# Splitting the second product's result straight from PSUM, with a scale bounded ahead of time

## The chip, the core and the metric

The kernel runs on one core of a Trainium2 chip. The metric is the device time of one execution in microseconds (us); the kernel before took 1235.76 us, the median of three timed runs (1233.34 to 1237.47).

The engines of the core are TensorE (PE in the profile; its weight loads are PEld), VectorE (DVE), ScalarE (ACT), GpSimd (POOL) and SyncE (SP, which issues nearly all DMAs here). Each has a queue of its own that it works through in order.

## The reference: what is computed

Attention over 4 batches of 448 tokens with 12 heads of 64, and on its output two gated products one after the other, 1792 tokens in all. The inputs are float64 for the weights and fp32 accuracy is wanted of the result.

```
q_n, k_n = rmsnorm(q, g_q), rmsnorm(k, g_k)
attn = softmax(q_n @ k_n^T / 8)
x = (attn @ v), heads side by side           # [1792, 768]

a = x @ w_a                                  # [1792, 1536]
b = x @ w_b
y = (a * b) @ w_out                          # [1792, 768]      <- the second product

h = y @ w2_in                                # [1792, 2048]
g = max(h, 0) + alpha * min(h, 0)
out = g @ w2_out                             # [1792, 768]
```

## The kernel before

**Split products.** PE multiplies in fp16. To keep fp32's accuracy, every operand is stored as two fp16 halves, hi and lo, after scaling by a power of two; a product is three matmuls (`prod`, L746): hi by hi, hi by lo, lo by hi. Each matmul here is 128x128 by 128x448. Weights are split the same way once (`w_load`, `w_convert`, `w_scale`, `w_split`, L618 to L710) as they are first used, their halves stored to a scratch tensor in HBM, and loaded from there in later batches. `w_scale` takes a weight chain's sum of squares and derives from it a power-of-two scale and its inverse; the inverses of all six chains of `w_out` stand in `inv["y"]`, a [128, 6] tile.

**Stages.** Work goes in stages, one letter for the product and one digit for the batch: `a` (x by w_a and w_b, 24 chains), `y` (a*b by w_out, 6 chains of 36 matmuls in two halves), `h` (y by w2_in, 16 chains of 18 matmuls) and `o` (g by w2_out, 6 chains). The order is a0 y0 h0 o0 a1 y1 a2 h1 o1 y2 a3 h2 y3 o2 h3 o3. So only y0 is followed directly by the stage that needs its result; after y1, y2 and y3 another stage comes in between. Attention of the next batch is woven into these stages at fixed rates (`RATE`); its score matmuls write tile `s`, its output matmuls tile `x`. The first batch's stages also convert and split the weights. A tile framework's scheduler arranges the instructions on each engine.

**The second product, `stage_y` (L809 to L835).** A chain's sum is in a PSUM tile `ps` from `new_ps()` (three buffers in turn). After the chain's second half ACT copies it to an fp32 tile in SBUF, scaled by the weight's inverse scale (L820), and squares that into a bf16 tile `sq` (L821). When all six chains are done, PE multiplies a matrix of ones by the six squares (L827), which adds the squares over all rows, into a PSUM tile `norm`. DVE takes the maximum over the tokens (L829) and derives the batch's scale `sy` and its inverse `iy` with three small integer operations (`power`, L109 to L120). Only then `split` (L758) makes the halves of each chain m: ACT the hi half, `Copy` with scale `sy` (L760), and DVE the lo half, `t * sy - hi` (L761). Before h0 the six splits follow at once; in the other batches they are put on the list `tasks` and taken one by one in the next stage (`next_w`).

**What uses it.** `stage_h` reads `Y[b, kk]`; its first chain needs all six. In `stage_o` GpSimd multiplies the inverse scales together into `cum` (L892 to L895), among them `iy` of the batch.

**A similar scale.** `h_scales` (L682) already does for w2_in's chains what the change now does for w_out's too: it takes the largest of the inverse scales as one common scale, so that the halves of `g` can be made as soon as a chain is done (flag `state["cgf"]`).

Of the kernel before, what the change touches and what calls it, by code (L numbers as in the profile page):

```python
# [19 lines left out]
def attention_gated_mlps_kernel(  # L20
# [15 lines left out]
    nc = tc.nc  # L36
# [32 lines left out]
    def slot32(name):  # L69
        return slot_p.tile([128, S], F32, tag="slot", name=name)  # L70
# [10 lines left out]
    gT = const.tile([128, 1], F32, name="gT")  # L81
    gkT = const.tile([128, 1], F32, name="gkT")
    ones = const.tile([128, 128], F32, name="ones")
    onesb = const.tile([128, 128], BF16, name="onesb")
    gbc = const.tile([128, D], F32, name="gbc")
    gkb = const.tile([128, D], F32, name="gkb")
    gm = const.tile([128, 1], F32, name="gm")
# [3 lines left out]
    cg = const.tile([128, 1], F32, name="cg")  # L91
    icg = const.tile([128, 1], F32, name="icg")
    cgf = const.tile([128, KF2], F32, name="cgf")
    ssv = const.tile([KP, B, NP], F32, name="ssv")
    ssab = const.tile([128, 2, KF], F32, name="ssab")
    sx, ix, sab, iab, sy, iy, cum = [
        const.tile([128, B], F32, name=n) for n in ("sx", "ix", "sab", "iab", "sy", "iy", "cum")
    ]
    inv = {
        "a": const.tile([128, 2 * KF], F32, name="inv_a"),  # L100
# [5 lines left out]
    def mm(o, a, b, first, last):  # L106
        nc.tensor.matmul(out=o, lhsT=a, rhs=b, start=first, stop=last)  # L107
# [42 lines left out]

    def setup0():
        nc.vector.memset(ones, 1.0)
        nc.vector.memset(onesb, 1.0)
        for t in p16:
            nc.vector.memset(t, 0.0)

# [376 lines left out]
        )  # L533
        P[g] = None

    state = dict(pin=True, cgf=False)
    preps = (prep2, prep3, prep4)
    preps_f = (prep2f, prep3f, prep4f)

# [126 lines left out]
    def w_scale(u):  # L666

        if u not in squares:
            return
        kind, n, part = stream[u]  # L670
        _, parts, _ = CHAINS[kind]
        chains = GROUP[kind]
        us = range(u - parts * chains + 1, u + 1)
        sc = sm_p.tile([128, 2], F32, tag="sc", name="sc")[:, 0:chains]
        iv = inv[kind][:, n - chains + 1:n + 1]
        power(total(squares.pop(u), len(us), chains), sc, iv)
        for x in us:
            scales[x] = sc[:, (x - us[0]) // parts:(x - us[0]) // parts + 1]
        if (kind, n) == ("h", KF2 - 1):
            h_scales()  # L680

    def h_scales():  # L682

        mx = sm_p.tile([128, 1], F32, tag="mh", name="mh")
        ci = sm_p.tile([128, 1], F32, tag="mh", name="ci")
        nc.vector.tensor_reduce(out=mx, in_=inv["h"], axis=AX.X, op=ALU.max)
        nc.vector.tensor_scalar(
            ci.bitcast(I32), mx.bitcast(I32), -1.0, float(254 << 23), op0=ALU.mult, op1=ALU.add
        )
# [68 lines left out]
    def split(t, s, name):  # L758
        x = slot(name)
        nc.scalar.activation(out=x[:, 0], in_=t, func=AF.Copy, scale=s)  # L760
        nc.vector.scalar_tensor_tensor(  # L761
            out=x[:, 1], in0=t, scalar=s, in1=x[:, 0], op0=ALU.mult, op1=ALU.subtract
        )
        return x
# [42 lines left out]
            tasks.extend((lambda i=i: one(i)) for i in range(n))  # L807

    def stage_y(b):  # L809
        raw, sq = {}, [slot_p.tile([128, 2, S], BF16, tag="slot", name=f"sq{b}_{i}") for i in range(KD // 2)]  # L810
        for m in range(KD):
            ps = new_ps()[:, 0:S]
            for kh in range(2):
                yield
                hw = unit()
                for kk in range(KD):
                    prod(ps, hw, kk, AB[b, kh * KD + kk], kh + kk == 0, kh == 1 and kk == KD - 1)
                if kh == 1:
                    raw[m] = t = slot32(f"y32_{b}_{m}")
                    nc.scalar.activation(out=t, in_=ps, func=AF.Copy, scale=inv["y"][:, m:m + 1])  # L820
                    nc.scalar.activation(out=sq[m // 2][:, m % 2], in_=t, func=AF.Square)  # L821
                next_w()
        for f in range(KF):
            AB.pop((b, f))
        ps = ps_x.tile([128, 512], F32, tag="x", name="norm")[:, 0:S]
        for m in range(KD):
            mm(ps, onesb, sq[m // 2][:, m % 2], m == 0, m == KD - 1)  # L827
        t = sm_p.tile([128, 1], F32, tag="mx", name="mx")
        nc.vector.tensor_reduce(out=t, in_=ps, axis=AX.X, op=ALU.max)  # L829
        power(t, sy[:, b:b + 1], iy[:, b:b + 1])  # L830

        def one(m):
            Y[b, m] = split(raw.pop(m), sy[:, b:b + 1], f"y{b}_{m}")

        after(stages_after("y", b) == "h", one, KD)  # L835

    def stage_h(b):
        raw = {}
# [30 lines left out]
    def stage_o(b):  # L869
        NT, PT = 4, S // 4  # L870
        k = CHAINS["o"][2]

        def finish(m, ps):
            t = tmp()

            nc.scalar.activation(  # L876
                out=t.rearrange("q (p c) -> q c p", c=NI),
                in_=ps.rearrange("q (c p) -> q c p", c=NI),
                func=AF.Copy, scale=inv["o"][:, m:m + 1],
            )  # L880
            po = new_ps()[:PT].rearrange("p (t f) -> p t f", t=NT)
            for i in range(NT):
                nc.tensor.transpose(po[:, i, :], t[:, i * PT:(i + 1) * PT], ident)  # L883
            ob = ob_p.tile([PT, NT, 128], F32, tag="ob", name="ob")
            nc.scalar.activation(out=ob, in_=po, func=AF.Copy, scale=cum[:PT, b:b + 1])
            nc.sync.dma_start(
                out=out[b * S:(b + 1) * S, m * 128:(m + 1) * 128].rearrange("(t p) f -> p t f", t=NT),
                in_=ob,
            )

        c = cum[:, b:b + 1]
        nc.gpsimd.tensor_tensor(c, ix[:, b:b + 1], iab[:, b:b + 1], op=ALU.mult)  # L892
        nc.gpsimd.tensor_tensor(c, c, iy[:, b:b + 1], op=ALU.mult)
        nc.gpsimd.tensor_tensor(c, c, icg, op=ALU.mult)
        nc.gpsimd.tensor_tensor(c, c, ix[:, b:b + 1], op=ALU.mult)  # L895
        late = None
        for m in range(KD):
            ps = new_ps()[:, 0:S]
            for part in range(4):
                yield  # L900
                hw = unit()
                for kk in range(k):
                    prod(
                        ps, hw, kk, G[b, part * k + kk],
                        part + kk == 0, part == 3 and kk == k - 1,
                    )
# [93 lines left out]
```

## Time and profile before

| | |
|---|---|
| timed, median of 3 | 1235.76 us (1233.34 to 1237.47) |
| profiled execution: time | 1237.6 us |
| profiled execution: span from first to last instruction | 1235.8 us |
| mean granted TensorE clock | 0.981 |
| 24 squares, L821, ACT | 576 ns each (median) |
| 24 norm matmuls, L827 by way of L107, PE | 352 ns each as modelled; their starts are closer |
| 4 maxima, L829, DVE | 623 ns each (median) |

A matmul's row gives a duration from its start to its modelled end, while the next one starts well before that; what a matmul costs in a stream is the distance from start to start. "Idle before" in a timeline row is the time the engine stood still before it, with what released it. A stretch is given by its limits in us from the span's start.

### The profile page before, as it was taken

The page shows a single profiled execution, that of the slowest core. Times are in us where ns is not written, and L with a number is a line of the kernel's source. Part 1 is how long each engine was busy: PE and PEld are TensorE (multiplying, and loading weights), DVE is VectorE, ACT ScalarE, POOL GpSimd, SP SyncE. Part 2 cuts the span into 40 slices and gives each one's busy share as a digit, 9 for nine tenths or more (in the row PEclk, how much of TensorE's full clock was granted, in tenths as well). Part 3 has the DMA queues.
Part 4 walks back from the last instruction along what each step waited for, and adds up shares of the span by engine and source line. Part 5 has one row for each costly group of instructions (what it writes and reads, how often), then busy time and mean ns, then how long its engine had stood idle before and what let it go on. Part 6 is the DMA issues. An engine that isn't in the chain of part 4 may idle for free.

```text
span 1235.8 us, 18195 instructions
## 1 busy us (share of the span) xinstructions
PE 1169.1 (95%) x6574; PEld 599.5 (49%) x6574; DVE 677.4 (55%) x1455; ACT 738.8 (60%) x1504; POOL 10.4 (1%) x32
## 2 busy tenths in 40 slices
PE   6997998989988999979999999999999999999998
PEld 4553554444534444435455454545555555554554
DVE  7898999889899667666551465331111440102400
ACT  7998999999889767676643465553221441213311
POOL 1000000000000000000000000000000000000000
PEclk9997999999999999989999999999999999999999
DMA  7558999999999999897854737876333333344343
GB/s 196 162 169 214 306 338 323 298 299 304 287 262 287 238 253 240 190 225 166 219 145 125 167 104 170 191 189 158 102 116 116 115 117 107 110 144 129 98 128 89
DMA packets 311243, 234.68 MB, mean 190 GB/s; under 512 B 175440, under 2 KB 284496, under 8 KB 311152
## 3 DMA queue, kind: packets, MB, share of 16 engines
q1 hardware_dynamic: 311040, 233.43, 71.7%
q8 instruction: 52, 0.85, 0.3%
q0 software_dynamic: 112, 0.07, 0.2%
q14 instruction: 39, 0.32, 0.1%
HBM read 155.79 MB, written 32.24 MB: 152 GB/s over the span
## 4 chain that ended last, share of the span: by engine, by line
PE 54%; DMA 2%; ACT 1%; DVE 1%; issue 0%; SPq 0%; ACTq 0%; DVEq 0%
PE p L107 49%; PE s L107 2%; PE x L107 2%; DMA pT<-p 2%; PE p L883 1%; ACT t L876 0%; PE norm L107 0%; ACT p L479 0%; ACT pf L434 0%; DVE nm L417 0%; SPq L486 0%; DVE ab L782 0%; DVE p L480 0%; DVE kr L332 0%; DVE qr L326 0%
## 5 line engine op out<-in xcount | busy, mean ns | idle before, releaser
L107 PEld LDWEIGHTS <-w 128*128 128x128 f16 x4896 | 476.7, 99 | 477.0 <-issue 49.7
L107 PE MATMUL p<-x,w 128*128 128x448 f16 x1728 | 336.8, 354 | 2.1 <-ACT t L779 2.0
L107 PE MATMUL p<-g,w 128*128 128x448 f16 x1152 | 229.5, 356 | 5.5 <-DVE g L844 2.1
L107 PE MATMUL p<-y,w 128*128 128x448 f16 x1152 | 224.7, 356 | 3.5 <-ACT y L760 3.2
L107 PE MATMUL p<-ab,w 128*128 128x448 f16 x864 | 170.8, 358 | 1.3 <-ACT ab L760 1.3
L417 DVE TENSOR_REDUCE nm<-s 128x2 f32<-128x896 f32 x84 | 91.1, 1085 | 41.7 <-PE s L107 41.3
L480 DVE SCALAR_TENSOR_TENSOR p<-pf,ri,p 128x448 f16<-128x448 f32 x126 | 84.4, 680 | 34.3 <-ACT p L479 34.0
L479 ACT ACTIVATE p<-pf,ri 128x448 f16<-128x448 f32 x126 | 81.4, 663 | 36.0 <-DMA pT<-p 28.1
L434 ACT ACTIVATE pf<-s,nm,esc 128x448 f32<-128x448 f32 x126 | 90.1, 719 | 1.3
L858 DVE SCALAR_TENSOR_TENSOR t<-t,al,p 128x448 f32<-128x448 f32 x55 | 37.3, 678 | 96.5 <-ACT t L857 96.5
L782 DVE SCALAR_TENSOR_TENSOR ab<-p,inv_a,t 128x448 f32<-128x448 f32 x48 | 32.5, 677 | 96.0 <-PE p L107 95.9
L706 DVE SCALAR_TENSOR_TENSOR w<-wf,sc,w 128x768 f16<-128x768 f32 (+1 forms) x76 | 70.2, 926 | 4.5 <-ACT w L705 4.1
L876 ACT ACTIVATE t<-p,inv_o 128x448 f32<-128x448 f32 x24 | 25.6, 1067 | 76.4 <-PE p L107 76.4
L785 ACT ACTIVATE junk<-ab 128x448 bf16<-128x448 f32 x48 | 27.4, 572 | 68.0 <-DVE ab L782 68.0
L650 DVE SCALAR_TENSOR_TENSOR wf<-raw,wf 128x768 int32<-128x768 int32 (+1 forms) x76 | 65.8, 867 | 0.5
L705 ACT ACTIVATE w<-wf,sc 128x768 f16<-128x768 f32 (+1 forms) x76 | 65.5, 866 | 0.0
L644 ACT ACTIVATE wf<-raw 128x768 f32<-128x768 f32 (+1 forms) x76 | 63.3, 838 | 1.6 <-DVE w L706 1.2
L658 ACT ACTIVATE junk<-wf 128x768 bf16<-128x768 f32 (+1 forms) x76 | 58.9, 775 | 2.9 <-DVE wf L650 2.5
L857 ACT ACTIVATE t<-p 128x448 f32<-128x448 f32 x55 | 29.7, 541 | 48.4 <-PE p L107 48.2
L843 ACT ACTIVATE g<-t,cgf 128x448 f16<-128x448 f32 x55 | 36.7, 668 | 34.6 <-DVE t L858 34.6
L107 PE MATMUL s<-kT,qT 128*64 128x448 f16 x252 | 50.2, 376 | 6.1 <-ACT pf L434 2.8
L844 DVE SCALAR_TENSOR_TENSOR g<-t,cgf,g 128x448 f16<-128x448 f32 x55 | 37.5, 682 | 29.6 <-ACT g L843 29.5
(140 smaller groups left out, 1065.1 us busy)
## 6 DMA issues: line engine op xcount, KB each, us to landing
w<-sc_a SPq DMA_DIRECT2D x72, 384.0 KB, 3.2
w<-sc_h SPq DMA_DIRECT2D x48, 384.0 KB, 3.0
w<-sc_o SPq DMA_DIRECT2D x72, 256.0 KB, 3.1
w<-sc_y SPq DMA_DIRECT2D x36, 384.0 KB, 3.2
raw<-in_moe_w_in_dram SPq DMA_DIRECT2D x16, 768.0 KB, 7.8
raw<-in_moe_w_out_dram SPq DMA_DIRECT2D x24, 512.0 KB, 5.9
raw<-in_moe_w_a_dram SPq DMA_DIRECT2D x12, 768.0 KB, 7.4
raw<-in_moe_w_b_dram SPq DMA_DIRECT2D x12, 768.0 KB, 7.5
```

The costliest lines, as they stand in the source:

```text
L107: nc.tensor.matmul(out=o, lhsT=a, rhs=b, start=first, stop=last)
L417: nc.vector.tensor_reduce(out=nm, in_=ps[:, :, 0:S], axis=AX.X, op=ALU.max, negate=True)
L434: nc.scalar.activation(out=pf, in_=ps[:, j, 0:S], func=AF.Exp, bias=nm[:, j:j + 1], scale=scale[j], accum_out=su[:, j:j + 1],)
L479: nc.scalar.activation(out=t[:, 0, :, 0:KP], in_=pf, func=AF.Copy, scale=r)
L480: nc.vector.scalar_tensor_tensor(out=t[:, 1, :, 0:KP], in0=pf, scalar=r, in1=t[:, 0, :, 0:KP], op0=ALU.mult, op1=ALU.subtract,)
L644: nc.scalar.activation(out=t, in_=hi.bitcast(F32), func=AF.Prelu, scale=2.0 ** -112, alpha=-(2.0 ** 32))
L650: nc.vector.scalar_tensor_tensor(out=ti, in0=lo, scalar=29, in1=ti, op0=ALU.logical_shift_right, op1=ALU.bitwise_or)
L658: nc.scalar.activation(out=junk(768, size(kind)), in_=t, func=AF.Square, accum_out=sums[0][:, j:j + 1])
L705: nc.scalar.activation(out=w[:, 0], in_=t, func=AF.Copy, scale=s)
L706: nc.vector.scalar_tensor_tensor(out=w[:, 1], in0=t, scalar=s, in1=w[:, 0], op0=ALU.mult, op1=ALU.subtract)
L844: nc.vector.scalar_tensor_tensor(out=x[:, 1], in0=t, scalar=cgf[:, f:f + 1], in1=x[:, 0], op0=ALU.mult, op1=ALU.subtract,)
L858: nc.vector.scalar_tensor_tensor(out=t, in0=t, scalar=al[:, f:f + 1], in1=ps, op0=ALU.mult, op1=ALU.add)
```

## The change

The batch's scale `sy` is no longer measured from y. `power` makes each scale from a norm, and the scales of a*b and of w_out's chains already bound the size of each sum in PSUM. So one constant factor 2^-17 and the ratio of each chain's inverse scale to the largest of them (`cyf`, [128, 6]) are enough to split, and `iy` is one [128, 1] value for all batches. `cyf` is made once, when the last of w_out's chains has its scale, which happens in the course of y0. From then on a chain's halves are taken from its PSUM tile as soon as the chain is done. The chains of y0 that end before that are copied to SBUF in fp32 (without scale) and split later, one beside each chain that follows. Squares, norm matmuls, their maximum, the tile `onesb` and the fp32 copies go.

```diff
@@ in w_scale
         if (kind, n) == ("h", KF2 - 1):
-            h_scales()
-
-    def h_scales():
+            ci, mx = common("h")
+            nc.vector.tensor_scalar(cgf, inv["h"], ci, cg, op0=ALU.mult, op1=ALU.mult)
+            nc.gpsimd.tensor_tensor(icg, icg, mx, op=ALU.mult)
+            state["cgf"] = True
+        if (kind, n) == ("y", KD - 1):
+            ci, mx = common("y")
+            nc.vector.tensor_scalar(cyf, inv["y"], ci, 2.0 ** -17, op0=ALU.mult, op1=ALU.mult)
+            nc.vector.tensor_scalar(iy, mx, 2.0 ** 17, None, op0=ALU.mult)
+            state["cyf"] = True
+
+    def common(kind):
 
         mx = sm_p.tile([128, 1], F32, tag="mh", name="mh")
         ci = sm_p.tile([128, 1], F32, tag="mh", name="ci")
-        nc.vector.tensor_reduce(out=mx, in_=inv["h"], axis=AX.X, op=ALU.max)
+        nc.vector.tensor_reduce(out=mx, in_=inv[kind], axis=AX.X, op=ALU.max)
         nc.vector.tensor_scalar(
             ci.bitcast(I32), mx.bitcast(I32), -1.0, float(254 << 23), op0=ALU.mult, op1=ALU.add
         )
-        nc.vector.tensor_scalar(cgf, inv["h"], ci, cg, op0=ALU.mult, op1=ALU.mult)
-        nc.gpsimd.tensor_tensor(icg, icg, mx, op=ALU.mult)
-        state["cgf"] = True
+        return ci, mx
@@ stage_y
-        raw, sq = {}, [slot_p.tile([128, 2, S], BF16, tag="slot", name=f"sq{b}_{i}") for i in range(KD // 2)]
+        raw = {}
+
+        def one(m):
+            Y[b, m] = split(raw.pop(m), cyf[:, m:m + 1], f"y{b}_{m}")
+
         for m in range(KD):
             ps = new_ps()[:, 0:S]
...
-                if kh == 1:
-                    raw[m] = t = slot32(f"y32_{b}_{m}")
-                    nc.scalar.activation(out=t, in_=ps, func=AF.Copy, scale=inv["y"][:, m:m + 1])
-                    nc.scalar.activation(out=sq[m // 2][:, m % 2], in_=t, func=AF.Square)
                 next_w()
+            if state["cyf"]:
+                raw[m] = ps
+                for x in sorted({m, min(raw)}):
+                    one(x)
+            else:
+                raw[m] = t = slot32(f"y32_{b}_{m}")
+                nc.scalar.copy(t, ps)
+        for x in sorted(raw):
+            one(x)
         for f in range(KF):
             AB.pop((b, f))
-        ps = ps_x.tile([128, 512], F32, tag="x", name="norm")[:, 0:S]
-        for m in range(KD):
-            mm(ps, onesb, sq[m // 2][:, m % 2], m == 0, m == KD - 1)
-        t = sm_p.tile([128, 1], F32, tag="mx", name="mx")
-        nc.vector.tensor_reduce(out=t, in_=ps, axis=AX.X, op=ALU.max)
-        power(t, sy[:, b:b + 1], iy[:, b:b + 1])
-
-        def one(m):
-            Y[b, m] = split(raw.pop(m), sy[:, b:b + 1], f"y{b}_{m}")
-
-        after(stages_after("y", b) == "h", one, KD)
@@ stage_o
-        nc.gpsimd.tensor_tensor(c, c, iy[:, b:b + 1], op=ALU.mult)
+        nc.gpsimd.tensor_tensor(c, c, iy, op=ALU.mult)
```

How the rows stand then, at two places. First DVE between y0 and h0. In the rows below `mx`, `pw`, `sy` and `iy` are the maximum of the norms and what `power` makes of it, `wf` is a weight being converted, `w` its halves, `qr` and `kr` are the attention's inputs of a later batch, `t`, `r` and `m` its row norms, `y_0` to `y_5` the halves of the six chains. Before:

```order
L829 TENSOR_REDUCE mx<-norm 128x1
L326 TENSOR_TENSOR qr<-qr,r 128x448
L332 SCALAR_TENSOR_TENSOR kr<-kr,r 112x512
L329 TENSOR_TENSOR qr<-qr,gbc 128x448
L114 TENSOR_SCALAR pw<-mx 128x1
L650 SCALAR_TENSOR_TENSOR wf<-raw,wf 128x768
L117 TENSOR_SCALAR sy<-pw 128x1
L120 TENSOR_SCALAR iy<-pw 128x1
L647 TENSOR_SCALAR wf<-wf 128x768
L114 TENSOR_SCALAR pw<-tot 128x2
L650 SCALAR_TENSOR_TENSOR wf<-raw,wf 128x768
L761 SCALAR_TENSOR_TENSOR y_0_3331<-y_0_0_2724,sy,y_0_3331 128x448
```

And after, up to the last of the six lo halves:

```order
L712 SCALAR_TENSOR_TENSOR w_3352<-wf,sc,w_3352 128x768
L259 TENSOR_TENSOR t<-r 128x30
L650 SCALAR_TENSOR_TENSOR wf<-raw,wf 128x768
L260 SCALAR_TENSOR_TENSOR t<-t,m 128x30
L115 TENSOR_SCALAR pw<-tot 128x2
L263 SCALAR_TENSOR_TENSOR r<-t,r 128x30
L647 TENSOR_SCALAR wf<-wf 128x768
L259 TENSOR_TENSOR t<-r 128x30
L118 TENSOR_SCALAR sc<-pw 128x2
L121 TENSOR_SCALAR inv_h<-pw 128x2
L260 SCALAR_TENSOR_TENSOR t<-t,m 128x30
L767 SCALAR_TENSOR_TENSOR y_5_3320<-p,cyf,y_5_3320 128x448
```

Before, all six lo halves stood behind the maximum and its scale, in a row of six of which the first is shown; after, `y_5` reads the PSUM tile `p`, the other five stand further ahead among y0's work, and the attention's `qr` and `kr` rows come behind it.

Second PE at the same hand-over. `ab` is a half of a*b, `w` a weight, `norm` and `onesb` the tiles of the norm, `s` the attention's scores, `tot` the sum of a weight's squares. Before, the end of the norm and the way to h0's first matmul, with most score rows in between left out by taking two pieces:

```order
L107 LDWEIGHTS onesb
L107 MATMUL norm<-sq_2_2649,onesb 128x448
L107 LDWEIGHTS qS
L107 MATMUL s<-kT,qS 64x448
L107 LDWEIGHTS onesb
L107 MATMUL norm<-sq_2_2649,onesb 128x448
L107 LDWEIGHTS qT
L107 MATMUL s<-kT,qT 64x448
```

```order
L107 LDWEIGHTS qS
L107 MATMUL s<-kT,qS 64x448
L107 MATMUL tot<-ss,ones 128x2
L107 LDWEIGHTS qS
L107 MATMUL s<-kT,qS 64x448
L107 LDWEIGHTS w_3196
L107 MATMUL p<-y_0_3331,w_3196 128x448
```

And after, y0's last matmul and h0's first:

```order
L108 LDWEIGHTS w_3143
L108 MATMUL p<-ab_11_2642,w_3143 128x448
L108 MATMUL tot<-ss,ones 128x2
L108 LDWEIGHTS w_3198
L108 MATMUL p<-y_0_2954,w_3198 128x448
```

The sixteen score matmuls (two steps of eight) that stood between y0 and h0 now stand behind h0's first chain and further on; h0's first chain of 18 follows y0 directly.

## Rows read from the trace of the kernel before

**Rows 1.** The page, part 1: busy us, share of the span, instructions.

```profile
PE 1169.1 (95%) x6574; PEld 599.5 (49%) x6574; DVE 677.4 (55%) x1455; ACT 738.8 (60%) x1504; POOL 10.4 (1%) x32
```

**Rows 2.** Busy time by stretch: length, then each engine's us (instructions), PEclk, DMA share, GB/s.

```profile
218.60:261.40 42.80, 39.99 (x221) 20.10 (x221) 35.59 (x67) 41.34 (x78) 0.24 (x1) 0.96 1.08 295
261.40:270.40 9.00, 9.00 (x54) 4.82 (x54) 8.72 (x22) 8.34 (x18) 0.00 (x0) 1.00 1.09 277
270.40:279.05 8.65, 4.37 (x27) 2.12 (x26) 8.63 (x24) 8.28 (x17) 0.37 (x1) 0.89 1.16 336
279.05:284.90 5.85, 5.81 (x18) 2.41 (x18) 5.83 (x11) 5.24 (x11) 0.00 (x0) 0.58 0.97 235
284.90:325.00 40.10, 40.10 (x232) 21.06 (x231) 34.58 (x65) 34.47 (x67) 0.00 (x0) 1.00 1.08 307
325.00:342.00 17.00, 16.78 (x95) 8.46 (x94) 17.00 (x40) 16.86 (x38) 1.61 (x3) 1.00 1.09 294
342.00:352.90 10.90, 6.55 (x35) 2.60 (x29) 10.76 (x19) 10.90 (x24) 0.00 (x0) 0.97 0.98 261
553.20:605.20 52.00, 52.00 (x300) 25.52 (x300) 34.62 (x75) 35.03 (x74) 0.00 (x0) 0.96 0.81 186
...
1017.70:1058.70 41.00, 41.00 (x218) 21.23 (x217) 1.36 (x2) 7.26 (x12) 0.00 (x0) 1.00 0.36 103
```

**Rows 3.** Timeline of PE, y0 to h0: start us, us, instruction, [idle before <-releaser].

```profile
270.58 0.38 PE L107 MATMUL s<-kT,qT 128*64 128x448 f16 x2
270.79 0.36 PE L107 MATMUL s<-kT,qS 128*64 128x448 f16 x2
...
271.45 1.12 PE L107 MATMUL norm<-sq,onesb 128*128 128x448 bf16 x5
...
279.09 6.16 PE L107 MATMUL p<-y,w 128*128 128x448 f16 x19 [3.23 <-ACT y L760]
```

**Rows 4.** Timeline of DVE at the same place.

```profile
261.42 1.09 DVE L417 TENSOR_REDUCE nm<-s 128x2 f32<-128x896 f32 x1 [0.60 <-PE s L107]
...
274.24 0.61 DVE L829 TENSOR_REDUCE mx<-norm 128x1 f32<-128x448 f32 x1
274.77 0.61 DVE L326 TENSOR_TENSOR qr<-qr,r 128x448 f32<-128x448 f32 x1
...
277.37 0.14 DVE L117 TENSOR_SCALAR sy<-pw 128x1 int32<-128x1 int32 x1
```

**Rows 5.** Tile y: count, duration ns min/median/max, first and last start, forms.

```profile
L820 ACT ACTIVATE y<-p,inv_y x24: 608/633/635, 227.8 to 1058.8; 128x448 f32<-128x448 f32 x24
L821 ACT ACTIVATE sq<-y x24: 559/576/578, 229.0 to 1059.4; 128x448 bf16<-128x448 f32 x24
L760 ACT ACTIVATE y<-y,sy x24: 652/654/668, 278.4 to 1064.3; 128x448 f16<-128x448 f32 x24
L761 DVE SCALAR_TENSOR_TENSOR y<-y,sy,y x24: 673/677/685, 279.1 to 1065.2; 128x448 f16<-128x448 f32 x24
```

**Rows 6.** The same view of tile x.

```profile
L530 ACT ACTIVATE x<-x,sx x6: 633/657/684, 38.0 to 122.1; 128x448 f16<-128x448 f32 x6
L531 DVE SCALAR_TENSOR_TENSOR x<-x,sx,x x6: 672/675/684, 38.9 to 123.1; 128x448 f16<-128x448 f32 x6
```

**Rows 7.** Timeline of PE after y1, at a2's start.

```profile
608.26 0.35 PE L107 MATMUL norm<-sq,onesb 128*128 128x448 bf16 x1 [1.38 <-ACT sq L821]
```

**Rows 8.** DVE's groups from 218 to 270: busy us, mean ns | idle before, releaser.

```profile
L706 DVE SCALAR_TENSOR_TENSOR w<-wf,sc,w 128x768 f16<-128x768 f32 x10 | 10.1, 1011 | 1.3 <-ACT w L705 1.0 <-DMA sc_y<-w 0.2
L650 DVE SCALAR_TENSOR_TENSOR wf<-raw,wf 128x768 int32<-128x768 int32 x10 | 9.6, 955 | 0.2
...
L647 DVE TENSOR_SCALAR wf<-wf 128x768 int32<-128x768 int32 x10 | 5.5, 553 | 1.2 <-ACT wf L644 1.2
```

**Rows 9.** SP's waits from 218 to 353: us in total, times, longest.

```profile
SPq L709 <- DVE w L706: 6.8, 3, 5.1
```

**Rows 10.** ACT's waits in y1, from 553 to 606.

```profile
ACT y L820 <- PE p L107: 2.4, 2, 1.9
```

More of the change, by code (lines that the diff above doesn't have):

```diff
@@ L83, in attention_gated_mlps_kernel @@
     ones = const.tile([128, 128], F32, name="ones")
-    onesb = const.tile([128, 128], BF16, name="onesb")
     gbc = const.tile([128, D], F32, name="gbc")
@@ L93, in attention_gated_mlps_kernel @@
     cgf = const.tile([128, KF2], F32, name="cgf")
+    cyf = const.tile([128, KD], F32, name="cyf")
+    iy = const.tile([128, 1], F32, name="iy")
     ssv = const.tile([KP, B, NP], F32, name="ssv")
     ssab = const.tile([128, 2, KF], F32, name="ssab")
-    sx, ix, sab, iab, sy, iy, cum = [
-        const.tile([128, B], F32, name=n) for n in ("sx", "ix", "sab", "iab", "sy", "iy", "cum")
+    sx, ix, sab, iab, cum = [
+        const.tile([128, B], F32, name=n) for n in ("sx", "ix", "sab", "iab", "cum")
     ]
@@ L152, in setup0 @@
         nc.vector.memset(ones, 1.0)
-        nc.vector.memset(onesb, 1.0)
         for t in p16:
@@ L534, in pv_out @@
         P[g] = None
-    state = dict(pin=True, cgf=False)
+    state = dict(pin=True, cgf=False, cyf=False)
     preps = (prep2, prep3, prep4)
```

## The prediction

> **What bounds the kernel now.** I read, in this order: the page's busy shares, the busy time by stretch, the idle places of TensorE (PE) in its timeline, and then the timelines of the two engines it waits for there. PE is busy 95% of the span, VectorE (DVE) 55%, ScalarE (ACT) 60% [rows 1]. So a matmul taken out of a stretch where PE never stops is worth its full time, and work taken off DVE or ACT is worth nothing unless PE waits for it there. The stretches differ, however [rows 2]. In stage y0 (218.6 to 270.4) ACT is busy 41.34 of 42.80 and then 8.34 of 9.00 us, DVE 35.59 and 8.72: both nearly full. From 270.40 to 279.05, where y0 hands over to h0, PE is busy only 4.37 of 8.65 us while DVE is busy 8.63. h0 (279.05 to 342) is PE-bound with the other two at 86 to 100%. At the start of o0 (342.00 to 352.90) PE is busy 6.55 of 10.90, and DVE (10.76) and ACT (10.90) are full: there PE waits for them. In y1 and y3 PE is busy the whole stretch and DVE has room (34.62 of 52.00 and 1.36 of 41.00).
>
> **The hand-over y0 to h0, as it is.** After y0's last product PE runs score matmuls of the attention, in pairs 0.2 us apart, and the six norm matmuls (five of them in 1.12 us, which is 0.19 each) [rows 3]. The maximum of the norms sits in DVE's queue until 274.24, its scale sy comes at 277.37 [rows 4], ACT's and DVE's splits follow, and h0's first matmul starts at 279.09 after 3.23 us of idle PE [rows 3]. The granted clock is 0.58 over 279.05 to 284.90 [rows 2], and the row at 279.09 shows 19 matmuls in 6.16 us, 0.32 each instead of 0.19 [rows 3]. So h0's first 18 matmuls end at 279.09 + 18 x 0.324 = 284.9; at the upper level (2.4 GHz) they would have ended at 282.5. The low level costs 2.4 us.
>
> **The change, part by part.**
>
> (1) The norm matmuls go: 24 x 0.19 = 4.5 us of PE. The six of y0 lie inside the hand-over and are counted there; the 18 of y1, y2 and y3 stand in stretches where PE does not pause ([rows 2] has the first and the last of the three), so 18 x 0.19 = 3.4 us is gained in full.
>
> (2) After y1 the last norm matmul waits 1.38 us for ACT's square, with a2's matmuls behind it on PE [rows 7]. That wait goes, and nothing replaces it: Y of batch 1 is needed only in h1, a whole stage later. 1.4 us.
>
> (3) ACT in y0: six squares (0.576) and four copies (0.633) go [rows 5], 6.0 us; the hi halves remain, read from PSUM. DVE: the 0.61 us reduction goes [rows 4], `common` adds four instructions of 0.15 or so and one of 0.3, about nothing in sum. **Price of a split read from PSUM.** The trace has no such row, but attention's output of batch 0 is the same form (PSUM in, fp16 out, a per-partition scale): hi 0.657, lo 0.675, against 0.654 and 0.677 from SBUF [rows 5, 6]. I take no difference. The Trainium skill (Perfetto Trace Analysis, Optimizing Scalar/DVE Operations) speaks against reading twice from PSUM: it gives DVE some 65 ns more per instruction there than from SBUF, and ACT some 42 ns less. By that rule DVE's four direct lo halves of y0 would come to 0.26 us more ahead of h0; the rows here do not show it.
>
> (4) Where the lo halves now stand. In y0 they move from the hand-over (six in a row on DVE, with ACT's six hi halves) to where each product ends. The last, y_5, is what h0 waits for. On DVE the order between the score reduction L417 (starts 261.42, [rows 4]) and y_5's lo holds 26 instructions: three weight lo halves of 1.01, two shift-ors of 0.955, two shifts of 0.553, two probability lo halves (0.68, the form of y's), one sum of squares (0.6), y_4 and y_5 themselves (0.68 each) and fourteen small ones of 0.15 to 0.18 [rows 5, 8]: 3.0 + 1.9 + 1.1 + 1.4 + 0.6 + 1.4 + 2.3 = 11.7 us; rows overlap by 0.08 or so (274.24 + 0.61 against 274.77, [rows 4]), which makes it 9.8. So y_5 is ready between 262.5 + 9.8 = 272.3 and 274.2, a microsecond later if DVE reaches L417 late (it has four more lo halves before it, 2.7 us, against 7.2 us of idle time in 218.60 to 261.40 [rows 2]). PE needs it after h0's first 15 matmuls: 270.6 + 15 x 0.19 = 273.4. h0's first 18 then end between 274.0 and 275.7 and owe the score matmuls that the order puts behind them, 8 pairs of 0.19 and one total, 1.8 us. Against 284.9 that is a gain of 7.4 to 9.1 us, of which 2.4 is clock; I take 8.3.
>
> (5) What is late next: the start of o0. PE waits there 10.90 - 6.55 = 4.35 us, because DVE and ACT are full from 325 on [rows 2]. They do not get 8.3 us lighter. What leaves their queues behind y0 is 5 lo halves and the norm's reduction and scale on DVE (3.4 + 1.0 = 4.4 us), and 5 hi halves, one copy and one square on ACT (4.5 us). The rest, 8.3 - 4.4 = 3.9 us, has to come out of their idle time in h0, which is 5.5 us on either (284.90 to 325.00: DVE 34.58, ACT 34.47 of 40.10, [rows 2]). Between nothing and 3.9 us is given back; I take 2.5, nearer the upper end, since some of that idle time is waits for transfers.
>
> (6) Added waits. DVE's lo now waits for ACT's hi, and that for the product; behind it on DVE stand weight and probability halves, on which the weight stores and the transposes in SP's queue wait. In y1 ACT's copy waited for PE twice, 2.4 us together [rows 10], and DVE has 17.4 us idle there [rows 2]: nothing. A PSUM bank is held for 1.3 us and a queue's length instead of 0.63; its next user comes three products later, 13 us in a y stage, 6.8 us where a2 follows: nothing. The scale iy, which GpSimd multiplies in, is there earlier; the slots that are freed were waited for by nobody.
>
> **The sum.** Hand-over 8.3, less 2.5 given back, plus 3.4 and 1.4: 10.6 us. The profiled run took 1237.6 us (span 1235.8), 1.8 above the median of the three timed runs; as a run like that the changed kernel gives 1227.0, as a median 1235.76 - 10.6 = 1225.2 us. With the ends of (4) and (5): 7.4 - 3.9 + 4.8 = 8.3 to 9.1 + 4.8 = 13.9, 1221.9 to 1227.5.
>
> **Rivals.**
>
> *Given back in full.* DVE, ACT and the transfers (mean share of the DMA engines 1.08 and 1.09 in y0 and h0, [rows 2], so they are never free) set the time up to 352.9, and o0's start waits as much longer as h0 comes earlier. Then only (1) and (2) stay, with up to 2 us of the rest: 4.8 to 6.8 us, 1229 to 1231. For it: the three are full from 325 to 352.9. Against it: 4.4 us of work really leaves their queues, and h0 has idle time.
>
> *More.* The lighter ACT and the missing idle stretch also end o0's waits of 4.35 us and a fall of the clock there (0.97 over that stretch): 9.1 + 4.8 + 3 to 5, 1217 to 1219. Against it: (5).
>
> *Slower.* SP's queue is in order, and its weight stores already waited for DVE's weight halves three times, 6.8 us in all, 5.1 at the longest [rows 9]; raw weight loads stand behind them. If a lo half holds DVE until its product is done, the store, the next load and then the weights are late, PE stops, and the clock falls as at 279: 3.2 + 2.4 = 5.6 us each time. Three such stops, in y0, h0 and o0, make 16.8 against 10.6, and the kernel takes 1242. It decides from two stops on (11.2 against 10.6). Against it: in y0 ACT reaches the products late rather than early, being full there [rows 2].
>
> *The scale is not there in time.* Were cyf ready only after y0, y0 would keep its copies. The order has it ahead of y0's third split, so at most two copies remain, as assumed.
>
> **How the numbers follow.** The forecast gets 0.63, given back in full 0.22, more 0.09, slower 0.06 (the last rival changes nothing). About 0.3%, 3.7 us, is what can be told from no change, so faster means below 1232.0. The forecast and the rival "more" lie wholly below; of "given back in full" I leave more than half there, as the timed runs scatter by 2 us: faster 0.85, within 0.3% 0.10, slower 0.05. Range: down to 1219, up to 1232, the worst of "given back" with a run's scatter; left out are "slower", some of "more" and a rest of "given back", under 0.2.
>
> **What would show it.** The idle time of 3.23 us before h0 under 1 us, and no stretch at clock 0.5 there; 24 rows of norm gone, and no wait of 1.4 us in a2; lo from PSUM 0.67 to 0.68; h0's first matmul at 270 to 272; o0's start with 4 to 8 us of idle PE, not less. It is wrong if h0's first product waits over 2 us for y_5's lo, if o0's start waits over 10 us, or if PE waits for weights in h0.

## The result, and the profile after

The changed kernel takes 1222.9 us, the median of four runs (1221.67 to 1225.36), against 1235.53 (1233.34 to 1237.47) for the kernel before on the same chip: ratio 0.9900, 95% interval 0.9885 to 0.9914, 12.6 us less. The prediction was 1225.2, with 1219 to 1232. The profiled execution took 1225.36 us (span 1223.6, granted clock 0.985). In a later series the same kernel (`e5_after_again`) took 1224.62, ratio 0.9919 [0.9902, 0.9936], 10.0 us less; the sum had been 10.6.

In the page's first part (answers to [rows 1]) PE has 24 matmuls fewer, ACT 24 us of work less, DVE 4 us less:

```profile
PE 1158.7 (95%) x6550; PEld 595.6 (49%) x6550; DVE 673.7 (55%) x1442; ACT 714.4 (58%) x1458; POOL 11.9 (1%) x32
```

PE's timeline at the end of y0 (answers to [rows 3]) goes from y0's last product straight to h0's first, with no idle time; the score matmuls `s` stand behind h0's first chain.

```profile
267.69 4.70 PE L108 MATMUL p<-ab,w 128*128 128x448 f16 x24
272.23 0.28 PE L108 MATMUL tot<-ss,ones 128*128 128x2 f32 x2
272.37 3.56 PE L108 MATMUL p<-y,w 128*128 128x448 f16 x18
275.86 0.38 PE L108 MATMUL s<-kT,qT 128*64 128x448 f16 x2
```

The first chain of 18 lasts 3.5 us, 0.19 per matmul, where it was 0.32 [rows 3]. DVE's timeline of the same place (answers to [rows 4]), with the lo halves of two chains:

```profile
263.28 1.09 DVE L417 TENSOR_REDUCE nm<-s 128x2 f32<-128x896 f32 x1 [0.40 <-PE s L108]
...
265.19 0.69 DVE L767 SCALAR_TENSOR_TENSOR y<-p,cyf,y 128x448 f16<-128x448 f32 x1 [0.23 <-ACT y L766]
...
273.64 0.68 DVE L767 SCALAR_TENSOR_TENSOR y<-p,cyf,y 128x448 f16<-128x448 f32 x1
```

The last of them, `y_5`, is done at 274.3, before the product that needs it comes at 272.37 + 15 x 0.19 = 275.2.

Busy time by stretch of the changed kernel, columns as in [rows 2]: the hand-over, h0 in three pieces, o0's start, y1, and a2's start.

```profile
272.40:275.86 3.46, 3.46 (x19) 1.62 (x19) 3.46 (x14) 2.52 (x5) 0.00 (x0) 1.00 1.10 361
275.86:300.00 24.14, 23.96 (x143) 12.75 (x144) 22.06 (x45) 22.23 (x42) 0.00 (x0) 1.00 1.13 299
300.00:325.00 25.00, 23.85 (x142) 12.17 (x139) 22.47 (x47) 22.00 (x47) 1.60 (x3) 1.00 1.13 306
325.00:337.20 12.20, 11.27 (x64) 5.54 (x62) 12.20 (x26) 12.20 (x27) 0.00 (x0) 1.00 1.12 340
337.20:348.50 11.30, 7.21 (x36) 3.21 (x37) 11.27 (x20) 11.30 (x25) 0.00 (x0) 0.93 1.08 287
547.60:597.90 50.30, 50.30 (x300) 25.00 (x299) 36.83 (x79) 32.28 (x69) 0.00 (x0) 0.99 0.81 189
597.90:604.00 6.10, 6.10 (x37) 2.94 (x36) 3.29 (x5) 2.93 (x6) 0.00 (x0) 1.00 0.99 205
```

The granted clock at the hand-over is 1.00, the upper level (2.4 GHz), where it was 0.58 [rows 2]. PE does not stop in a2's first 6.10 us, so the wait of [rows 7] is gone. h0, in which PE hardly stopped before, now loses 0.2 + 1.2 + 0.9 = 2.3 us, and o0's start still loses 11.30 - 7.21 = 4.1.

The trace's tile view of y (answers to [rows 5]) shows the new forms: 22 splits read PSUM (`p`), the two chains of y0 that ended before the scale was there are copied and read from SBUF.

```profile
L766 ACT ACTIVATE y<-p,cyf x22: 615/634/650, 249.2 to 1047.8; 128x448 f16<-128x448 f32 x22
L767 DVE SCALAR_TENSOR_TENSOR y<-p,cyf,y x22: 673/683/685, 250.4 to 1048.5; 128x448 f16<-128x448 f32 x22
L835 ACT COPY y<-p x2: 514/523/532, 229.1 to 236.6; 128x448 f32<-128x448 f32 x2
L766 ACT ACTIVATE y<-y,cyf x2: 664/668/672, 248.7 to 251.0; 128x448 f16<-128x448 f32 x2
L767 DVE SCALAR_TENSOR_TENSOR y<-y,cyf,y x2: 676/680/684, 249.8 to 251.7; 128x448 f16<-128x448 f32 x2
...
  DVE y L767: 58.5, 15
```

The last line, from the part on who waited for the tile: DVE stood idle 58.5 us in 15 waits for ACT's hi half. All but 1.5 us of that lies in y2 and y3, where DVE has little else to do; in y1, y2 and y3 PE is busy the whole stage (50.30 of 50.30 us in y1's row above, 46.84 of 46.84 from 823.26 in y2, 40.85 of 40.85 from 1006.75 in y3), so the waits cost PE nothing there.

**Lengths of the stages.** A stage is counted from its first matmul to the next stage's first, from the PE rows of one profiled execution each; the table gives the difference to the kernel before in us. "Head" is all ahead of y0, which the change does not touch.

| kernel | head | y0 | h0 | o0 | y0 to o0 | a1 | y1, a2 | h1, o1 | y2, a3 | y3, o2 |
|---|---|---|---|---|---|---|---|---|---|---|
| before, length | 218.6 | 60.5 | 63.7 | 93.4 | 217.6 | 116.9 | 142.7 | 137.1 | 129.9 | 100.6 |
| changed | +1.1 | -7.8 | +1.9 | +0.3 | -5.6 | -1.4 | -3.6 | 0.0 | -1.3 | -1.3 |
| e5_after_again | +2.9 | -9.2 | +0.9 | +3.7 | -4.6 | -2.6 | -2.6 | -1.4 | -1.3 | -1.3 |
| e2_y0_only | -0.3 | -9.7 | +0.7 | +1.5 | -7.5 | -1.7 | -1.0 | -1.9 | 0.0 | 0.0 |
| e1_late_only | +2.0 | -0.4 | -0.2 | +0.1 | -0.6 | +0.7 | -1.3 | +1.0 | -1.3 | -1.3 |
| e3_norms_back | -0.2 | -9.2 | +1.6 | +1.2 | -6.4 | -0.4 | -1.2 | -1.8 | -0.2 | -0.2 |
| e4_y0_copies | +0.7 | -5.9 | -1.8 | +0.5 | -7.2 | +0.5 | -3.3 | -2.1 | -1.3 | -1.3 |
| e6_copy_first | +0.7 | -9.9 | +2.0 | +2.5 | -5.3 | -0.9 | -1.3 | -1.9 | -1.3 | -1.3 |
| e7_before_filler | -0.5 | -1.6 | +2.2 | -1.1 | -0.5 | -1.4 | -0.8 | +1.5 | 0.0 | 0.0 |
| e8_after_relief | -0.3 | -10.2 | +3.2 | -4.0 | -11.0 | +7.6 | -2.6 | -1.8 | -1.3 | -1.3 |
| e9_before_relief | +0.2 | -1.9 | -0.7 | -5.4 | -8.0 | -1.4 | -0.3 | -1.7 | 0.0 | 0.0 |
| e10_more_in_y0 | +1.2 | -4.3 | +6.2 | -4.5 | -2.6 | +0.8 | -3.4 | -1.5 | -1.3 | -1.3 |
| e11_more_in_h0 | +0.8 | -9.1 | +12.2 | -6.0 | -2.9 | +2.7 | -2.8 | -1.8 | -1.3 | -1.3 |
| e12_less_in_y0 | +0.1 | -9.6 | -1.0 | +3.2 | -7.4 | +2.2 | -3.3 | -1.8 | -1.3 | -1.3 |

The head alone differs by up to 3.4 us between these executions, and h1 with o1 by 3.6; a few us of one profile are chance. The medians of 6 to 12 runs each decide, and the table says where. A profiled execution can also lie off its kernel's median: e1's took 1236.83 (median 1231.42), e12's 1224.78 (median 1228.44).

### The profile page after: what moved, and what is told of

It is laid out like the page before. It is cut to its first block, busy times and chain, and to the rows that moved or that the text cites. A ratio compares the mean times of both kernels' runs of the same rounds, so it can differ in the third digit from the quotient of the medians.

```text
span 1223.6 us, 18095 instructions
## 1 busy us (share of the span) xinstructions
PE 1158.7 (95%) x6550; PEld 595.6 (49%) x6550; DVE 673.7 (55%) x1442; ACT 714.4 (58%) x1458; POOL 11.9 (1%) x32
## 4 chain that ended last, share of the span: by engine, by line
PE 52%; DMA 1%; ACT 1%; DVE 1%; issue 0%; SPq 0%; ACTq 0%
PE p L108 48%; PE s L108 2%; PE x L108 2%; PE p L887 1%; DMA pT<-p 1%; DMA kr<-in_k_dram 0%; ACT t L880 0%; DMA qT<-q 0%; ACT pf L434 0%; ACT p L479 0%; DVE p L480 0%; DVE nm L417 0%; SPq L486 0%; DVE ab L788 0%; ACT x L530 0%
## 5 line engine op out<-in xcount | busy, mean ns | idle before, releaser
L862 DVE SCALAR_TENSOR_TENSOR t<-t,al,p 128x448 f32<-128x448 f32 x55 | 37.3, 678 | 100.6 <-ACT t L861 100.5
L644 ACT ACTIVATE wf<-raw 128x768 f32<-128x768 f32 (+1 forms) x76 | 63.7, 843 | 4.6 <-DMA raw<-in_moe_w_in_dram 2.7
L650 DVE SCALAR_TENSOR_TENSOR wf<-raw,wf 128x768 int32<-128x768 int32 (+1 forms) x76 | 65.8, 867 | 0.3
```

The source lines that it names most:

```text
L644: nc.scalar.activation(out=t, in_=hi.bitcast(F32), func=AF.Prelu, scale=2.0 ** -112, alpha=-(2.0 ** 32))
L650: nc.vector.scalar_tensor_tensor(out=ti, in0=lo, scalar=29, in1=ti, op0=ALU.logical_shift_right, op1=ALU.bitwise_or)
L862: nc.vector.scalar_tensor_tensor(out=t, in0=t, scalar=al[:, f:f + 1], in1=ps, op0=ALU.mult, op1=ALU.add)
```

## The experiments

Three series, each against its own runs of the kernel before: medians 1235.18 (e1 to e4), 1234.02 (e5 to e8) and 1234.2 (e9 to e12). The third ran on another chip than the first two and has no run of the changed kernel; where two kernels of different series are compared, it is by their ratios to the kernel before.

### The two halves of the change apart

`e1_late_only` measures batch 0's scale as before and bounds those of the others; `e2_y0_only` is the reverse. Both methods stand in the kernel, chosen by batch (e2 with `b > 0`):

```diff
-"y": stage_y
+"y": stage_ym if b == 0 else stage_y     # stage_ym: the body of before, with sym, iym
```

> Only y1, y2 and y3 are changed; y0 keeps its squares, norm matmuls, measured scale and splits behind them. My theory, that the gain is the sum of separate pieces (3.4 us for 18 norm matmuls, 1.4 us for the wait in a2, and the rest at the hand-over y0 to h0 and behind it): 4.8 us faster than before, 1230.7. Rival, that the hand-over is what counts and the late stages hide their norms: within 1.5 us of before. Second rival, that the measured excess over my forecast (12.6 against 10.6) comes from the late stages (clock in y1): 6 to 7 us faster.

1231.42 us, ratio 0.9978 [0.9959, 0.9996]: 2.7 us less, between 0.5 and 5.1. The stages say where: 1.3 each in y2 with a3, in y3 with o2, and in y1 with a2, and about nothing from y0 to o0. The interval holds both the 4.8 of the theory and the 1.5 of the first rival; it excludes the second rival's 6 to 7.

> Only y0 is changed; y1, y2 and y3 keep squares, norm matmuls and measured scale. Theory: 12.6 less 4.8, that is 6 to 8 us faster than before, 1228 to 1229.5, with h0's first matmul right behind y0's last as in the changed kernel. Rival (the hand-over's 8.3 us are given back in h0 and o0): 0 to 3 us faster.

1227.53 us, ratio 0.9939 [0.9917, 0.9962]: 7.5 us less (4.7 to 10.3). y0 to o0 is 7.5 us shorter, y2 and later stages are as before. The two halves add up to 10.2, and the whole change in `e5_after_again` gives 10.0: within intervals of over 2 us on each, they do not disturb each other.

> The changed kernel itself, on the same chip as the next three, as their reference. It should repeat its ratio of 0.990 to before, some 12 us; the theory's sum says 10.6, and if the excess of 2 us was chance of that session (the clock fell less often in a1 and y1), the ratio moves to 0.991 to 0.992.

1224.62, ratio 0.9919 [0.9902, 0.9936]: the case of the expectation in which the excess of the first session was chance.

### The norm matmuls put back

`e3_norms_back` is the changed kernel with 18 unused matmuls of the norm's size and their maximum behind y1, y2 and y3; their operand is there already, so they cost PE time and no wait.

```diff
+        if b:
+            ps = ps_x.tile([128, 512], F32, tag="x", name="norm")[:, 0:S]
+            for m in range(KD):
+                mm(ps, ones16, Y[b, m % 4][:, 0], m == 0, m == KD - 1)
+            t = sm_p.tile([128, 1], F32, tag="mx", name="mx")
+            nc.vector.tensor_reduce(out=t, in_=ps, axis=AX.X, op=ALU.max)
```

> The changed kernel with six matmuls of the norm's shape put back behind each of y1, y2 and y3, on halves that are long ready, and the maximum behind them, whose result nobody uses. Theory (PE does not pause there, each costs 0.19 us): 18 x 0.19 = 3.4 us slower than the changed kernel, 1226.3, and no wait in front of them. Rival (they hide): no difference, 1223.

1228.22 us, ratio 0.9949 [0.9931, 0.9967]: 3.7 us slower than the changed kernel by the ratios (e5_after_again), where 3.4 was expected. The two intervals still touch; the stages are what shows it: y2 with a3 and y3 with o2 get 1.1 us longer each, which is 6 x 0.19. The tile view of norm in this kernel:

```profile
L109 PE MATMUL norm<-y,ones x18: 349/352/353, 598.3 to 1049.3; 128*128 128x448 f16 x18
```

A matmul that PE does not stop for is worth its place in the stream, 0.19, and not its modelled 0.352.

### What of the hand-over is the scale, and what the reading from PSUM

`e4_y0_copies` lets all six chains of y0 be copied to SBUF and split only behind y0, with the known scale. `e6_copy_first` copies every chain to SBUF first and splits it right after that.

```diff
@@ e4
-            if state["cyf"]:
+            if state["cyf"] and b:
@@ e6
-                raw[m] = ps
+                raw[m] = t = slot32(f"y32_{b}_{m}")
+                nc.scalar.copy(t, ps)
```

> The changed kernel, but y0 copies all six chains to SBUF in fp32 and splits them in a row after its last chain, with the scale known ahead; so the hand-over loses squares, norm matmuls, maximum and scale, and keeps the six splits. Theory (what h0 waits for is DVE's and ACT's queue at the end of y0, where the norm's maximum stood, and then the row of splits): the first split can start some 4 to 6 us sooner than before, the row of splits itself costs 1.3 us before h0's first matmul and paces the first chain at 0.68 per lo half, 4.1 us against 3.4; 3 to 5 us slower than the changed kernel, 1226 to 1228. Rival (the norm's latency was all of it, splits hide): within 1 us of the changed kernel, 1223 to 1224.

1224.22 us, ratio 0.9921 [0.9904, 0.9939]: the same as the changed kernel, to about 2 us. Here my theory fell. ACT's timeline in e4 shows the last copy and the six hi halves in a row, and PE's the hand-over:

```profile
272.72 0.51 ACT L835 COPY y<-p 128x448 f32<-128x448 f32 x1
273.13 3.46 ACT L766 ACTIVATE y<-y,cyf 128x448 f16<-128x448 f32 x6
```

```profile
270.84 0.28 PE L108 MATMUL tot<-ss,ones 128*128 128x2 f32 x2
...
272.20 0.36 PE L108 MATMUL tot<-ss,ones 128*128 128x2 f32 x2 [0.20 <-DVE r L263]
272.87 0.38 PE L108 MATMUL s<-kT,qT 128*64 128x448 f16 x2 [0.32 <-ACT pf L434]
...
273.86 5.41 PE L108 MATMUL p<-y,w 128*128 128x448 f16 x26
```

The first hi half is ready and PE starts 1.1 us after the last copy began, and the attention's score matmuls fill most of that time. y0 gains 5.9 instead of 7.8 to 9.9, and h0 then runs 1.8 shorter instead of 0.7 to 2.0 longer. h0's first chain ends 58.2 us after y0's start, with all sixteen score matmuls done, where it took 66.3 before: 8.1 us sooner. What made the old hand-over long was that the scale had to come through PE, through DVE's queue and through three more instructions in it [rows 4]; that the six splits stand behind y0 costs the total nothing that these runs can tell.

> The changed kernel, but each chain is first copied to SBUF in fp32 and split from there at once: the scale is known ahead, and PSUM is read once. It adds 22 copies of 0.52 us on ACT and 0.5 us to the way of y_5. Theory (the gain is in the known scale, not in reading PSUM twice): 0 to 2 us slower than the changed kernel, through ACT in y0 and a longer wait for y_5. Rival (reading straight from PSUM is a good part of the gain, ACT being full in y0): 4 us slower or more.

1226.97 us, ratio 0.9938 [0.9918, 0.9959]: 2.4 us slower than the changed kernel by the medians, with intervals that overlap: near the theory's 0 to 2, not the rival's 4, and not clear of noise. 22 copies of 0.53 are 11.7 us of ACT, and most of that is hidden.

### Is a gain of PE alone kept?

`e7_before_filler` is the kernel before with 28 unused matmuls behind y0's norm, so that PE has no idle stretch there and the clock does not fall.

```diff
+        if b == 0:
+            pf = new_ps()[:, 0:S]
+            for j in range(28):
+                mm(pf, onesb, sq[j % 3][:, 0], j == 0, j == 27)
```

> The kernel before, with 28 matmuls of the norm's shape (5.3 us, onto a PSUM tile that nobody reads) put into the hand-over from y0 to h0, so that PE does not stand idle there. Theory (the clock at 1.2 GHz over h0's first matmuls comes from the idle stretch and costs 2.4 us): those 18 matmuls run at 0.19 instead of 0.32 us, and the kernel is 1 to 2.4 us faster than before although it does more work. Rival (the clock does not follow from it, or the fillers delay the scores): not faster, up to 3 us slower.

1234.94 us, ratio 1.0011 [0.9998, 1.0023]: no gain, as the rival said. The clock was restored, as PE's timeline and the busy time by stretch show (against [rows 2] and [rows 3]):

```profile
272.21 4.13 PE L108 MATMUL p<-sq,onesb 128*128 128x448 bf16 x21
...
277.79 6.79 PE L108 MATMUL p<-y,w 128*128 128x448 f16 x35
```

```profile
277.79:284.42 6.63, 6.63 (x37) 3.53 (x37) 6.63 (x11) 6.63 (x13) 0.00 (x0) 1.00 1.03 224
342.00:353.00 11.00, 7.06 (x37) 2.91 (x34) 10.99 (x20) 11.00 (x23) 0.00 (x0) 0.94 1.07 266
```

h0's first 18 matmuls end at 281.1 (one at 277.01 and 17 x 0.194 behind 277.79), 62.9 us after y0's start instead of 66.3. Eight of the sixteen score matmuls and a total, about 1.0 us, are still owed then, so at equal work the gain is 2.4 us: what the clock had cost. It is gone at o0's start (y0 and h0 together +0.6): PE now stands 2.9 us in h0, where it stood 0.4 before. The longest stop there:

```profile
325.69 1.10 PE L108 MATMUL p<-y,w 128*128 128x448 f16 x5 [1.47 <-DVE t L863]
```

o0's start loses 3.9 us again with DVE and ACT full. So a gain of PE at the hand-over was not kept here, where no work left the other engines.

### Is it VectorE that gives the time back?

Two kernels leave out the shift-or L650 for w2_in and w2_out (the lowest three mantissa bits of these weights): `e8_after_relief` is the changed kernel, `e9_before_relief` the one before.

```diff
+        if kind in "ay":
             nc.vector.scalar_tensor_tensor(
                 out=ti, in0=lo, scalar=29, in1=ti, op0=ALU.logical_shift_right, op1=ALU.bitwise_or
             )
```

> The changed kernel without the step that puts the lowest three bits of the float32 mantissa into the converted weights of w2_in and w2_out (40 instructions, some 32 us of DVE in y0, h0 and o0); those weights are then cut to 21 bits. Theory (h0 and the start of o0 give back 2.5 us because DVE is full): 2 to 6 us faster than the changed kernel, with less idle PE at o0's start (3.8 us now). Rival (transfers or ACT hold h0): within 1 us of the changed kernel.

1229.46 us, ratio 0.9957 [0.9941, 0.9973]: 4.7 us slower than the changed kernel by the ratios, so theory and rival both missed. Up to o0's end it is ahead (-11.0 against -5.6 and -4.6), then a1 takes 9 us more. PE's timeline in a1 shows where: its products wait for a half of a*b on DVE, and then for an input of the attention.

```profile
494.66 0.54 PE L108 MATMUL p<-x,w 128*128 128x448 f16 x2
499.11 4.88 PE L108 MATMUL p<-x,w 128*128 128x448 f16 x18 [3.90 <-DVE ab L789]
...
505.94 2.24 PE L108 MATMUL p<-x,w 128*128 128x448 f16 x11 [1.07 <-DMA qr<-in_q_dram]
```

After the stop, 18 matmuls take 4.88 us, 0.27 each, and the granted clock from 499.10 to 503.90 is 0.72: the clock falls too.

> The kernel before, with the same relief on VectorE as the last run had: the shift-or of 0.955 us that puts the lowest three mantissa bits into the fp32 weights is left out for w2_in and w2_out, so these weights lack those bits. Theory (VectorE is full from y0 to o0's end, with or without the change; PE that gets ahead there meets the attention's transposes later): y0, h0 and o0 together get 5 to 6 us shorter, a1 gives 7 to 10 back, the total is 3 to 6 us slower than the kernel before. Rival (the loss in a1 needs the change, which lets PE run further ahead than the attention can follow): the total is 3 to 6 us faster than the kernel before.

1227.09 us, ratio 0.9947 [0.9928, 0.9967]: 6.5 us faster than the kernel before by the ratio (4.1 to 8.9). The theory missed and the rival (3 to 6 faster) holds: y0 to o0 is 8.0 us shorter and a1 gives nothing back. Nor was VectorE the only limit. Busy time by stretch of e9, its y0, h0 and o0:

```profile
218.90:277.40 58.50, 52.38 (x296) 26.64 (x296) 45.56 (x106) 55.41 (x108) 0.49 (x2) 0.97 1.09 299
277.40:340.40 63.00, 63.00 (x350) 31.74 (x349) 54.46 (x108) 61.21 (x124) 0.62 (x3) 0.97 1.09 308
340.40:428.40 88.00, 78.58 (x462) 38.73 (x461) 65.78 (x149) 79.54 (x172) 0.00 (x0) 0.98 1.09 278
```

DVE's sum is 165.8 us here and 189.1 in the same three stages before, 23 us less, for a gain of 8: ACT is at 95, 97 and 90%, and in h0 PE never stops. I read this as three engines and the transfers (DMA share 1.09) in balance there, so that relieving one passes the bound to the next; no run shows it for each of them.

### The attention moved between the stages

Three versions of the changed kernel with other rates, to see whether the room that the change makes can be used:

```diff
-    RATE = {"a0": 4, "y0": 5, "h0": 4, "o0": 8, ...
+    RATE = {"a0": 4, "y0": 6, "h0": 4, "o0": 7, ...      # e10
+    RATE = {"a0": 4, "y0": 5, "h0": 5, "o0": 7, ...      # e11
+    RATE = {"a0": 4, "y0": 4, "h0": 4, "o0": 9, ...      # e12
```

> The changed kernel with three steps of the attention moved from o0 to y0 (rates 6 and 7 instead of 5 and 8). Theory (VectorE and ScalarE are full over the whole stretch from y0 to o0's end, so work moved inside it only changes where PE waits): y0 gets 2 to 4 us longer, o0 as much shorter, the total stays within 2 us of the changed kernel. Rival (the change made room in y0, and o0 waits for the attention's transfers): 2 to 4 us faster than the changed kernel.

1227.73 us, ratio 0.9955 [0.9938, 0.9973].

> The changed kernel with three steps of the attention moved from o0 to h0 (rates 5 and 7 instead of 4 and 8). Theory: as for the steps moved to y0, within 2 us of the changed kernel, with h0 2 to 4 us longer and o0 as much shorter. Rival (h0's idle time on VectorE, 5 us, can be filled): 2 to 4 us faster than the changed kernel.

1229.02 us, ratio 0.9949 [0.9931, 0.9967].

> The changed kernel with three steps of the attention moved from y0 to o0 (rates 4 and 9 instead of 5 and 8). Theory: within 2 us of the changed kernel, y0 2 to 4 us shorter, o0 as much longer. Rival (o0 is the tighter stage of the two): 2 to 4 us slower than the changed kernel.

1228.44 us, ratio 0.9953 [0.9936, 0.9971].

All three are 3.7 to 4.4 us slower than the changed kernel by the ratios, across series and chips, so for e10 and e11 both the theory (within 2) and the rival (faster) missed, and e12 agrees with its rival in size, but with e10 slower as well, not with its reason. Each trace shows a stop of PE that is longer than the changed kernel's at that place or that it does not have. In PE's timelines of e10 (h0), e11 (end of h0) and e12 (a1):

```profile
320.27 0.38 PE L108 MATMUL tot<-ss,ones 128*128 128x2 f32 x2 [2.46 <-ACT junk L658]
```

```profile
341.10 0.57 PE L108 MATMUL x<-pT,v 112*64 112x448 f16 x4 [3.30 <-DMA sc_h<-w]
```

```profile
501.09 3.48 PE L108 MATMUL p<-x,w 128*128 128x448 f16 x10 [3.01 <-DVE ab L788]
```

e10's waits for a weight's square on ACT, e11's behind a weight store, e12's in a1 where e8 lost its time. These are single stops in one trace each, and e12's profiled execution was as fast as the changed kernel, so they are not shown to be what the medians lost. No version tried beats the changed kernel; e4 equals it.

## Why the prediction was right, step by step

**Hand-over, 8.3 (7.4 to 9.1).** From y0's start to the end of h0's first chain, with 1.8 us for the score matmuls still owed, it is 275.86 + 1.8 - 219.72 = 57.9 us, against 284.9 - 218.63 = 66.3: 8.4. `y_5` was ready at 274.3, which is 54.6 us after y0's start, in the middle of the predicted 53.7 to 55.6 (272.3 to 274.2 on the trace of before), and held nobody up. By the same working e2, e3 and e5, whose first chain runs as undisturbed, give 9.7 to 10.2, over the upper end; the term was sized about a microsecond low. Where the lo halves stand, which part (4) worked out, did not matter as far as these runs can tell: e4 leaves all six behind y0 and its hand-over is 8.1 us shorter too.

**Given back, 2.5 (0 to 3.9).** That something is given back held, and e7 shows it alone: PE's gain is lost by o0's start where no work leaves the queues. The place was only half right. The prediction looked for longer waits at o0's start; those are as before (4.1 against 4.35 us). Over the whole of o0, though, PE stands 15.3 us where it stood 12.5, and new are stops in h0, at the totals of a weight's squares, behind a split of the attention's output on DVE and a square on ACT, in PE's timeline of the changed kernel:

```profile
306.04 0.38 PE L108 MATMUL tot<-ss,ones 128*128 128x2 f32 x2 [1.15 <-DVE x L531]
...
329.97 0.39 PE L108 MATMUL tot<-ss,ones 128*128 128x4 f32 x2 [0.76 <-ACT junk L658]
```

In size, the hand-over's gain less the difference of y0 to o0 is 8.4 - 5.6 = 2.8 here and 2.7 to 5.1 in e2, e3 and e5, so 2.5 was low by about as much as the gain was; that the two misses cancel is luck. What is left at o0's end, 4.6 to 7.5 in the five traces (with e6) and 7.5 in e2's timing, was predicted as 5.8.

The working behind the 2.5 does not hold. It let PE keep what leaves the queues behind y0, 4.4 us on DVE and 4.5 on ACT. In e4 the six splits stay there, so about 1 us leaves DVE's queue and less leaves ACT's, and still y0 to o0 is 7.2 us shorter. Another reading fits e4, e7 and the changed kernel: what counts is the work that ACT no longer does at all, the squares above all. Busy time from y0's start to o0's end, of the kernel before, the changed kernel, e4 and e7 in turn:

```profile
218.63:436.22 217.59, 197.52 (x1103) 97.86 (x1103) 189.13 (x400) 197.01 (x403) 2.18 (x5) 0.96 1.07 283
219.72:431.67 211.95, 190.89 (x1099) 96.12 (x1098) 187.72 (x400) 192.54 (x392) 2.72 (x5) 0.98 1.10 289
219.34:429.70 210.36, 193.29 (x1098) 96.48 (x1098) 187.31 (x398) 193.36 (x395) 3.11 (x5) 0.97 1.10 291
218.17:435.27 217.10, 201.21 (x1131) 100.19 (x1131) 188.73 (x400) 197.19 (x403) 2.58 (x5) 0.97 1.07 283
```

ACT is busy 197.0 and 197.2 us in the two that keep nothing, 192.5 and 193.4 in the two that do. But work removed is not always gained one for one (e9: 23 us of DVE for 8), and no run has the known scale with the squares kept. So how much of the kept gain comes from the earlier scale and how much from ACT's lighter load stays open.

**Norm matmuls, 3.4, and the wait in a2, 1.4.** y2 with a3 and y3 with o2 give 1.3 each in every kernel without norms (6 x 0.19 = 1.14 expected), and e3 takes 1.1 back. The wait at 608.26 [rows 7] is gone. y1 with a2, where 1.14 + 1.4 = 2.5 was expected, scatters: the nine kernels without norms there give 1.3 to 3.6, 2.7 in the mean, and the four that have them with their wait (before, e2, e7, e9) 0 to 1.0, 0.5 in the mean. The difference, 2.2, is near the 2.5. e1 as a whole gives 2.7 [0.5, 5.1] for 4.8.

**The price of reading PSUM.** Taken as no difference. The lo half takes 683 ns from PSUM and 680 from SBUF (684 for e6's 24), the hi half 634 and 668 (668 for e6's 24). The Trainium skill (Perfetto Trace Analysis, Optimizing Scalar/DVE Operations) gives DVE an overhead about 65 ns higher on PSUM than on SBUF and ACT one about 42 ns lower, as engine-busy times of which it calls profiled durations about twice. The traces agree in direction for ACT (34 ns less in the profiled rows) and show no such difference for DVE (3 ns more, or 1 less by e6).

**Added waits, nothing.** Held: 58.5 us of DVE waiting for hi halves, and no stop of PE in y1, y2 or y3.

**Rivals.** Given back in full: for the hand-over not so, as e2 gives 7.5. More: o0's waits did not end. Slower: SP's waits for a weight's lo half in y0 to o0's start were three and 6.8 us before [rows 9]; in the changed kernel's trace (219 to 349) these stores (L715) wait three times, 8.3 us, and twice an issue of the attention's transposes (L486) does:

```profile
SPq L715 <- DVE w L712: 8.3, 3, 4.3
SPq L486 <- DVE w L712: 7.8, 2, 4.8
```

PE did not stop for it: from y0's start to o0's start no stop is over 2 us but one in y0 that waits for a transpose of k (2.55 us at 259.01), and the kernel before has the same one there (2.55 us at 257.65).

**The rest, 12.6 against 10.6.** The first session's excess lies in a1 (-1.4, none expected) and in y1 with a2 (-3.6 for 2.5); e7, which changes nothing in these stages, shows -1.4 and -0.8 there. `e5_after_again` gives 10.0. I take the 2 us as chance; no run names another cause.

**Still open.** How much of the kept gain is ACT's lighter load, as said above. And why the relieved kernel loses 9 us in a1 with the change and none without it (e8, e9). PE gets to a1 11 us earlier in e8 and 8 in e9, so being early alone does not explain it. The path of the stop can be read: in e8 and e12 alike the half of a*b stands on DVE behind the attention's k (L352), that waits for ACT's cast of k (L343), and that for a transpose by DMA (1.23 us in e8, after 2.92 for q's; 3.24 in e12). But the cast waits 2.54 us in e9 too, and there PE does not stop.

## What to carry over

A scale that a bound gives ahead of time takes a round trip through three engines' queues out of the only place where the next stage waits, and the splits may then stand behind the stage or be read from PSUM at the same total (e4). Where two or three engines are nearly full, do not count the gap on PE alone: e7 won 2.4 us there and kept nothing, and the kernels that kept a gain there had also taken work from ACT. Where PE never stops, a removed matmul is worth about its distance to the next start (1.1 to 1.3 us for six of them here), not its modelled length.

## What was not expected of the hardware

DVE reads a 128x448 fp32 operand from PSUM as fast as from SBUF in this form (683 and 680 ns). ACT's plain copy from PSUM to fp32 takes 523 ns (e6: 532), where the form of before, with a per-partition scale, took 633 [rows 5]: a tenth of a microsecond more. And executions differ in a stretch that the change does not touch: from the start to y0's first matmul it is 219.7 and 221.5 us in two executions of the changed kernel, and 218.2 to 221.5 over all these kernels.
